# A wait for GpSimd behind VectorE at their shared port, with new durations for the planner and other banks for scores

## The chip, the cores and the metric

The kernel runs on one core of a Trainium2 chip. Five engines work side by side, each on its own queue of instructions: PE (TensorE) multiplies, DVE (VectorE), ACT (ScalarE) and POOL (GpSimd) do elementwise work, SP (SyncE) issues DMAs. The metric is the device time of one execution in microseconds (us); the kernel before took 814.11 us, the median of three runs (812.26 to 815.49).

## The reference

Attention with a causal window of 64 positions over 4 x 8 heads of 576 positions, then a mixture of 4 experts over the 2304 rows that come out. All of it is fp32.

```python
scores = scale * np.matmul(q, k.transpose(0, 1, 3, 2))        # q, k, v: (4, 8, 576, 64)
mask = (rel >= 0) & (rel < window)                            # rel = row - column, window = 64
attn = exp(where(mask, scores, -1e9) - max) / (sum + 1e-9)
x = (attn @ v).transpose(0, 2, 1, 3).reshape(2304, 512)
p = domain_probs / (domain_probs.sum(-1, keepdims=True) + 1e-9)   # (2304, 4)
for e in range(4):                                            # w1: (4, 512, 1024), w2: (4, 1024, 512)
    h = np.maximum(x @ w1[e], 0.0)
    out += p[:, e:e + 1] * (h @ w2[e])
```

## The kernel before, in words

The 2304 rows are cut into 3 groups of 768 rows, and a group's rows into 6 blocks of 128 for attention. The experts' hidden columns are cut into 16 units of 256, so that there are 48 pairs of group and unit (unit 0 to 47). Every fp32 operand of a large product is split in two, a rounded part (`hi`, a cast) and the remainder (`lo`, a subtraction), and three matmuls of the parts stand for one. The remainder is an operation with two inputs from SBUF; it is what DVE and POOL share between them.

The first product of a unit (x times w1) is done as seven products of quarter blocks instead of eight (P1 to P7, six matmuls of 384 columns each, L995), on sums and differences of quarters: B11, B21, B22 and T1 to T4 of a group. Group 0 starts with two units without that (`d`, L1071). The second product (h times w2) is plain in group 0 (`y`, L1189); in groups 1 and 2 it runs over pairs of units with seven products again (tiles `m8P` to `m22P`, L1106), whose weights `wp` are split by ACT (L698) and POOL (L701) and whose inputs `hs` are split at L886 and L889. The last pair is plain again (`z`, L1154).

Attention for a group runs beside the experts of the group before; group 0's attention is the start of the kernel. For a block: scores (`sb`, L367), the row maximum on DVE, the exponentials on ACT, the reciprocal on DVE (tile `st`, L427 and L428), the normalisation (tile `sm`, L434) on POOL or DVE, a transpose (on PE in group 0, by DVE's 32x32 transpose, L455, and a DMA through DRAM later), the product with v (`vb`, L493), and a copy into `xr` (L506).

Order. Nothing is scheduled by hand: each piece of work is a `Step` with a planned duration for every engine that may do it, a due time, the steps that it needs and the buffers that it takes. `Planner.order` plays the steps against these durations, gives each an engine, a start and a buffer, and emits them in order of start. PE's order is mostly fixed beforehand (`seq`). Steps that list an engine under `port` are planned so that DVE and POOL are never at the port at once (`port_free`), but in the program nothing holds POOL to this: a POOL instruction starts as soon as its own inputs are there and POOL is free. An instruction of DVE or POOL keeps its place in its engine's queue.

In PSUM there are eight banks b0 to b7. A score tile of group 0 may take b5, b6, b7, b3, b4, b0 or b1 (kind `pa0`), and the accumulators of the `d` products b0, b1 or b4 (kind `D`). While PE would stand idle by the plan in the first 60 us, filler matmuls (`warm_out`, L1270) are put in, one for each 0.35 us of planned gap.

## Time and profile before

| | us |
|---|---|
| median of 3 runs | 814.11 |
| the profiled execution, whole | 813.13 |
| its span, first to last instruction | 811.3 |
| PE busy / DVE / ACT / POOL in the span | 794.5 / 645.0 / 413.8 / 457.2 |
| mean granted clock of TensorE, as a share | 0.993 |

The profiled execution is 1.0 us below the median, and 1.8 us of it lie outside the span. Times in rows are counted from the span's start. A busy time is the union of an engine's instructions; a matmul's row ends later than the next one's start, since they are pipelined, so the distance of starts shows PE's pace.

### The profile page before, as it was taken

What the parts mean: (1) busy time and instruction counts of PE and PEld (TensorE: products, weight loads), DVE (VectorE), ACT (ScalarE), POOL (GpSimd) and SP (SyncE); (2) the same over time, 40 slices, a digit from 0 to 9 for tenths busy, and PEclk for the clock granted to TensorE, in tenths of its full rate; (3) what the DMA queues carried; (4) which work ended last, traced back from release to release, by engine and by line L of the source; (5) the groups of instructions that cost most, each with busy time, mean ns of one, the idle gap of its engine ahead of it and who ended that gap; (6) DMA issues with size and microseconds to landing.
All of it is one profiled execution on the core that took longest, in us unless ns stands there. A gap on an engine that the chain in (4) does not pass through costs nothing.

```text
span 811.3 us, 14972 instructions
## 1 busy us (share of the span) xinstructions
PE 794.5 (98%) x5256; PEld 746.9 (92%) x5261; DVE 645.0 (79%) x1097; ACT 413.8 (51%) x1031; POOL 457.2 (56%) x426
## 2 busy tenths in 40 slices
PE   8999999999999999999999999998899999999998
PEld 6888988888888888999999999988899999999998
DVE  5897666565756798888988987998899888878884
ACT  6866544454535454665766566584434333334320
POOL 4456867757555234546555544654355767776750
PEclk9999999999999999999999999998999999999999
DMA  9928889888776548786786767564485565655522
GB/s 333 294 80 281 320 283 332 283 286 275 254 269 223 187 169 288 252 278 216 254 278 206 237 220 242 169 201 144 148 271 177 200 198 187 215 191 191 178 84 78
DMA packets 106795, 181.93 MB, mean 224 GB/s; under 512 B 12849, under 2 KB 53217, under 8 KB 106721
## 3 DMA queue, kind: packets, MB, share of 16 engines
q1 hardware_dynamic: 106576, 180.59, 67.5%
q8 instruction: 41, 0.67, 0.3%
q10 hardware_dynamic: 144, 0.39, 0.1%
q14 instruction: 34, 0.27, 0.1%
HBM read 132.16 MB, written 48.78 MB: 223 GB/s over the span
## 4 chain that ended last, share of the span: by engine, by line
PE 88%; DVE 9%; ACT 2%; issue 1%; ACTq 0%; DVEq 0%
PE Y L995 17%; PE y L1189 16%; PE X L995 11%; PE V L995 11%; PE z L1154 2%; PE vb L493 2%; PE sb L367 2%; PE m13P L1106 2%; PE m9P L1106 2%; PE m10P L1106 2%; PE m12P L1106 2%; PE m8P L1106 2%; PE m22P L1106 2%; PE m20P L1106 2%; PE m18P L1106 2%; PE m19P L1106 2%
## 5 line engine op out<-in xcount | busy, mean ns | idle before, releaser
L701 POOL TENSOR_TENSOR wp_P<-wr_P,wp_P 128x512 fp32r<-128x512 f32 x105 | 148.9, 1429 | 77.5 <-ACT wp_P L698 66.9
L1189 PE MATMUL y<-w2s,h 128*128 128x512 f32 x576 | 148.9, 395 | 0.0
L1189 PEld LDWEIGHTS y<-w2s,h 128*128 128x128 f32 x576 | 106.4, 188 | 18.1 <-issue 0.9
L1017 ACT COPY u<-Y 128x384 f32<-128x384 f32 x92 | 44.1, 479 | 123.5 <-PE Y L995 111.5
L698 ACT CAST wp_P<-wr_P 128x512 fp32r<-128x512 f32 x105 | 65.2, 621 | 2.5 <-PE y L1189 1.5
L1014 DVE TENSOR_TENSOR c<-V,u 128x384 f32<-128x384 f32 x46 | 25.8, 561 | 46.9 <-ACT u L1017 46.3
L804 POOL TENSOR_TENSOR w2s<-w2r,w2s 128x512 fp32r<-128x512 f32 x33 | 46.5, 1420 | 23.8 <-ACT w2s L801 21.6
L434 POOL TENSOR_TENSOR sm<-sm,st 128x512 f32<-128x512 f32 x29 | 31.1, 1073 | 50.5 <-DVE st L428 48.3
L995 PE MATMUL Y<-T,w1a 128*128 128x384 f32 x276 | 57.1, 341 | 2.2 <-DVE T L596 1.5
L995 PE MATMUL Y<-T,w1c 128*128 128x384 f32 x276 | 56.7, 340 | 0.9 <-ACT u L1017 0.9
L995 PE MATMUL Y<-T,w1b 128*128 128x384 f32 x276 | 56.5, 341 | 0.6 <-ACT u L1017 0.6
L995 PE MATMUL X<-B,w1c 128*128 128x384 f32 x276 | 56.8, 341 | 0.0
L995 PE MATMUL V<-T,w1b 128*128 128x384 f32 x276 | 56.3, 339 | 0.5 <-DVE h L871 0.5
L995 PE MATMUL X<-B,w1a 128*128 128x384 f32 x276 | 55.5, 335 | 0.2 <-DVE w1a L773 0.2
L995 PE MATMUL V<-B,w1d 128*128 128x384 f32 x276 | 55.6, 336 | 0.2 <-DVE c L1014 0.2
L995 PEld LDWEIGHTS Y<-T,w1a 128*128 128x128 f32 x276 | 48.3, 188 | 5.7 <-DVE T L596 2.2
L995 PEld LDWEIGHTS Y<-T,w1c 128*128 128x128 f32 x276 | 49.6, 191 | 2.7 <-ACT u L1017 1.6
L995 PEld LDWEIGHTS Y<-T,w1b 128*128 128x128 f32 x276 | 49.2, 191 | 2.6 <-ACT u L1017 1.1
L995 PEld LDWEIGHTS V<-T,w1b 128*128 128x128 f32 x276 | 49.1, 188 | 2.3 <-DVE h L871 0.9
L995 PEld LDWEIGHTS X<-B,w1c 128*128 128x128 f32 x276 | 49.7, 191 | 1.4
L995 PEld LDWEIGHTS V<-B,w1d 128*128 128x128 f32 x276 | 48.9, 188 | 1.7 <-DVE c L1014 0.5
L995 PEld LDWEIGHTS X<-B,w1a 128*128 128x128 f32 x276 | 48.6, 188 | 0.5 <-DVE w1a L773 0.5
(583 smaller groups left out, 1973.5 us busy)
## 6 DMA issues: line engine op xcount, KB each, us to landing
wr_P<-kw_P SPq DMA_DIRECT2D x60, 256.0 KB, 4.0
w1a<-kw1a SPq DMA_DIRECT2D x30, 512.0 KB, 4.4
w1b<-kw1b SPq DMA_DIRECT2D x30, 512.0 KB, 3.8
w1c<-kw1c SPq DMA_DIRECT2D x30, 512.0 KB, 3.7
wr_P<-in_moe_w_dram SPq DMA_DIRECT2D x45, 256.0 KB, 4.3
w2r<-in_moe_w_dram SPq DMA_DIRECT2D x36, 256.0 KB, 4.4
vn<-in_v_dram SPq DMA_DIRECT2D x35, 256.0 KB, 5.0
kw1a<-w1a SPq DMA_DIRECT2D x16, 512.0 KB, 3.8
```

Source lines behind the costliest of these rows:

```text
L367: nc.tensor.matmul(ts[i][x * W : (x + 1) * W, p, :], qb.tile[lo:hi, p, x * W : (x + 1) * W], kt.tile[lo:hi, p, x * W : x * W + 2 * W], sta ...
L434: (nc.gpsimd if on == "POOL" else nc.vector).tensor_tensor(out=sm.tile, in0=sm.tile, in1=rl.to_broadcast([P, NP, P]), op=ALU.mult)
L493: nc.tensor.matmul(t[lo:hi, p, x * W : (x + 1) * W], vns[x].tile[:, p * P + lo : p * P + hi], pt_head, start=True, stop=True,)
L698: nc.scalar.copy(make(b, f"wp{pair}_{x}")[:, :, 0], r.tile)
L701: (nc.gpsimd if on == "POOL" else nc.vector).tensor_tensor(out=b.tile[:, :, 1], in0=r.tile, in1=b.tile[:, :, 0].bitcast(F32), op=ALU.subtract)
L804: (nc.gpsimd if on == "POOL" else nc.vector).tensor_tensor(out=b.tile[:, 1], in0=raw.tile, in1=b.tile[:, 0].bitcast(F32), op=ALU.subtract)
L995: nc.tensor.matmul(t[:, :T], wb.tile[:, a, wi, ws], cb.tile[:, x, c, :], start=first and m == 0, stop=m == 5, skip_group_check=True,)
L1014: return lambda on, t, p_: nc.vector.tensor_tensor(out=t, in0=p_, in1=o.tile, op=ALU.add)
L1017: (nc.vector.tensor_copy if on == "DVE" else nc.scalar.copy)(t, p_)
L1106: nc.tensor.matmul(o[:, :T], ww.tile[:, u, a, c * P : (c + 1) * P], hs[i, pname].tile[:, x], start=m == 0 and not onto, stop=m == 5, skip_ ...
L1154: nc.tensor.matmul(o[:, cols], w2p[i][f].tile[:, a, dq * P : (dq + 1) * P], hs[i, name[f, t_]].tile[:, x, cols], start=first and m == 0, s ...
L1189: nc.tensor.matmul(o, hh[:, a, ts], w[:, b], start=x == 0 and m == 0, stop=x == 1 and m == 5)
```

## The change

Four things change. (1) The planned durations: the scores' step on PE goes from 0.55 to 1.15 us, the product with v from 0.62 to 1.25, POOL's splits from 1.2 or 1.25 to 1.29, POOL's other operations and DVE's casts by some hundredths, so that the planner makes another order. (2) The scores of group 0's blocks 3 to 5 take banks of a new kind `pah`: b5, b6, b7 and b4. (3) Where POOL's step at the port was planned later than a DVE step at the port, POOL's first instruction of it now waits until that DVE step has ended. The DVE step taken is the last one whose planned end lies 0.3 us or more ahead of the POOL step's planned start, and the wait is made only if that end is later than the time at which the POOL step's own inputs were planned to be ready. (4) To know the instructions, `nc` is wrapped (`Core`, `Watch`); every DVE and POOL instruction of the kernel then carries the wrapper's line, L34. The arithmetic stays as it was.

```diff
+class Watch:
+    def __init__(self, engine):
+        self.engine, self.made = engine, []
+    def __getattr__(self, name):
+        f = getattr(self.engine, name)
+        def call(*a, **kw):
+            i = f(*a, **kw)
+            self.made.append(i)
+            return i
+        return call
...
+    slots["pah"] = slots["pa"] + ["b4"]
...
     def dvec(n):
-        return 0.1 + 0.00056 * n
+        return 0.13 + 0.00056 * n
     def pool_(n):
-        return 0.1 + 0.00215 * n
+        return 0.18 + 0.00216 * n
...
-        vns, sbs = [Buf(f"vn{n}") for _ in range(2)], [Buf(f"pa{n}") for _ in range(2)]
+        vns, sbs = [Buf(f"vn{n}") for _ in range(2)], [Buf("pah" if n == 0 and 2 * j >= GPB else f"pa{n}") for _ in range(2)]
...
-        s = add(f"S{u}", dict(PE=0.55 + 0.15 * pe_mask), scores, due, [q_dma, k_dma, t_step.get(2 * u - 2) if n else None], sbs, [qb, kt])
+        s = add(f"S{u}", dict(PE=1.15 + 0.2 * pe_mask), scores, due, [q_dma, k_dma, t_step.get(2 * u - 2) if n else None], sbs, [qb, kt])
...
-            l = add(f"wl{pair}{x}", dict(POOL=1.2), lo, due + 0.1, [h], [], [r, b], port=("POOL", "DVE"))
+            l = add(f"wl{pair}{x}", dict(POOL=1.29), lo, due + 0.1, [h], [], [r, b], port=("POOL", "DVE"))
...
+        first = len(nc.gpsimd.made)
+        del nc.vector.made[:]
         s.emit(s.engine)
+        if s.engine == "DVE" and s.port and nc.vector.made:
+            ended.append((s.done, nc.vector.made[-1]))
+        if s.engine == "POOL" and s.port:
+            while len(ended) > 1 and ended[1][0] <= s.start - AHEAD_OF_POOL:
+                ended.pop(0)
+            if ended and ended[0][0] <= s.start - AHEAD_OF_POOL and ended[0][0] > s.ready:
+                tc.add_manual_dep(
+                    nc.gpsimd.made[first].ins, ended[0][1].ins.name, mybir.DependencyInfo(mybir.DependencyClass.Sync, mybir.DependencyReason.DATA),
+                    reason="GpSimd takes its turn at the port",
+                )
...
+AHEAD_OF_POOL = 0.3
```

Of POOL's 400 steps at the port 196 get such a wait: 72 of the 105 `wp` splits, 44 of the weights' sums, the rest spread over the others. Of the DVE steps waited for, 91 are `hs` splits and 20 are DVE's 32x32 transposes. PE's order keeps 687 of its 709 steps in place; what moves is some scores and products with v, and the count of fillers, 22 before and 15 after.

POOL's queue where group 2 begins, before: the end of unit 31's splits, the weights `wp` of pairs 15 and 16, and unit 32's differences (`t32`).

```order
L889 TENSOR_TENSOR hs31P5_7092<-t31P5_7069,hs31P5_7092 128x384 [waits PE_49,Activation_49]
L701 TENSOR_TENSOR wp15_P7_6963<-wr15_P7_6875,wp15_P7_6963 128x2x256 [waits DMAHW0_49]
L701 TENSOR_TENSOR wp15_P5_7048<-wr15_P5_6931,wp15_P5_7048 128x2x256 [waits DMAHW1_49]
L701 TENSOR_TENSOR wp15_P6_7098<-wr15_P6_6986,wp15_P6_7098 128x2x256 [waits DMAHW4_49,PE_49,Activation_49]
L701 TENSOR_TENSOR wp15_P2_7130<-wr15_P2_7041,wp15_P2_7130 128x2x256 [waits DMAHW7_49,PE_49,Activation_49]
L914 TENSOR_TENSOR t32P7_7246<-r3200_7179,r3210_7221 128x384 [waits DVE_49]
L914 TENSOR_TENSOR t32P6_7276<-r3200_7179,t32P5_7263 128x384 [waits DVE_49,Pool_49]
L701 TENSOR_TENSOR wp15_P4_7177<-wr15_P4_7107,wp15_P4_7177 128x2x256 [waits DMAHW2_49,PE_49,Activation_49]
L701 TENSOR_TENSOR wp16_P1_7232<-wr16_P1_7154,wp16_P1_7232 128x2x256 [waits DMAHW3_49,PE_49,Activation_49]
```

The same place of POOL's queue after the change (all rows have the wrapper's line).

```order
L34 TENSOR_TENSOR hs31P7_7066<-t31P7_7051,hs31P7_7066 128x384 [waits DVE_49,PE_49]
L34 TENSOR_TENSOR wp15_P7_6943<-wr15_P7_6864,wp15_P7_6943 128x2x256 [waits DMAHW0_49,DVE_49]
L34 TENSOR_TENSOR wp15_P5_7015<-wr15_P5_6918,wp15_P5_7015 128x2x256 [waits DMAHW1_49,DVE_49,PE_49]
L34 TENSOR_TENSOR wp15_P6_7097<-wr15_P6_6975,wp15_P6_7097 128x2x256 [waits DMAHW4_49,PE_49,Activation_49]
L34 TENSOR_TENSOR wp15_P2_7116<-wr15_P2_7030,wp15_P2_7116 128x2x256 [waits DVE_49,DMAHW7_49,PE_49,Activation_49]
L34 TENSOR_TENSOR t32P6_7259<-r3200_7170,t32P5_7228 128x384 [waits DVE_49]
L34 TENSOR_TENSOR wp15_P4_7167<-wr15_P4_7087,wp15_P4_7167 128x2x256 [waits DVE_49,DMAHW2_49,PE_49,Activation_49]
L34 TENSOR_TENSOR wp16_P1_7223<-wr16_P1_7144,wp16_P1_7223 128x2x256 [waits DMAHW3_49,DVE_49,PE_49]
```

The `wp` splits stand in the same order, and five of the six now wait for DVE too: `wp15_P7` for the end of the second `T4` split, `wp15_P5` for `B22`, `wp15_P2` for `t32P7`, `wp15_P4` for the `hs32P4` split, `wp16_P1` for the `hs32P6` split. The difference `t32P7` has gone from POOL to DVE.

DVE's queue at the same place, before: the last splits of unit 31 and the splits of group 2's quarters, of which PE needs `T2` first.

```order
L914 TENSOR_TENSOR t31P4_7109<-r3101_7067,t31P6_7090 128x384 [waits DVE_49,Activation_49]
L889 TENSOR_TENSOR hs31P7_7080<-t31P7_7064,hs31P7_7080 128x384 [waits Activation_49]
L1120 TENSOR_TENSOR M1P30_4244<-m15P30_7100,M1P30_4244 128x384 [waits PE_49]
L889 TENSOR_TENSOR hs31P4_7119<-t31P4_7109,hs31P4_7119 128x384 [waits Activation_49]
L889 TENSOR_TENSOR hs31P6_7096<-t31P6_7090,hs31P6_7096 128x384
L596 TENSOR_TENSOR T2_2_6978<-T2d0_6802,T2_2_6978 128x384
L596 TENSOR_TENSOR T2_2_6978<-T2d1_6815,T2_2_6978 128x384
L596 TENSOR_TENSOR T3_2_7004<-xr2_4474,T3_2_7004 128x384 x2
```

And after:

```order
L34 TENSOR_TENSOR M1P30_4195<-m15P30_7080,M1P30_4195 128x384 [waits PE_49]
L34 TENSOR_TENSOR t31P4_7107<-r3101_7061,t31P6_7091 128x384 [waits DVE_49]
L34 TENSOR_TENSOR hs31P5_7078<-t31P5_7063,hs31P5_7078 128x384 [waits Activation_49]
L34 TENSOR_TENSOR hs31P6_7105<-t31P6_7091,hs31P6_7105 128x384 [waits Activation_49]
L34 TENSOR_TENSOR hs31P4_7119<-t31P4_7107,hs31P4_7119 128x384 [waits Activation_49]
L34 TENSOR_TENSOR T1_2_6907<-T1d1_6814,T1_2_6907 128x384
L34 TENSOR_TENSOR B21_2_6932<-xr2_4417,B21_2_6932 128x768
L34 TENSOR_TENSOR T2_2_6965<-T2d0_6935,T2_2_6965 128x384
L34 TENSOR_TENSOR T2_2_6965<-T2d1_6947,T2_2_6965 128x384
```

One split of unit 31 has changed places with POOL's (`hs31P7` against `hs31P5`), and the second `T1` split and the `B21` split, which stood earlier on DVE, now stand directly ahead of `T2`.

POOL's queue near the start, where the weights of unit 1 are split, before:

```order
L434 TENSOR_TENSOR sm2_1_483<-sm2_1_483,st2_1_415 128x512 [waits DVE_49]
L773 TENSOR_TENSOR w1c_0_512<-rc0_299,w1c_0_512 128x512 [waits DMAHW6_49,Activation_49]
L560 COPY gate_71<-B21_0_673 1x1 [waits DVE_49]
L773 TENSOR_TENSOR w1a_1_522<-ra1_302,w1a_1_522 128x512 [waits DMAHW7_49,Activation_49]
L773 TENSOR_TENSOR w1c_1_544<-rc1_303,w1c_1_544 128x512 [waits DMAHW0_49,Activation_49]
```

And after:

```order
L34 TENSOR_TENSOR w1c_0_534<-rc0_299,w1c_0_534 128x512 [waits DMAHW6_49,Activation_49]
L34 TENSOR_TENSOR tw0P5_663<-w2r01_390,w2r00_388 128x256 [waits DMAHW2_49,DMAHW1_49]
L34 COPY gate_71<-B21_0_667 1x1 [waits DVE_49]
L34 TENSOR_TENSOR w1a_1_538<-ra1_302,w1a_1_538 128x512 [waits DMAHW7_49,DVE_49,Activation_49]
L34 TENSOR_TENSOR w1c_1_558<-rc1_303,w1c_1_558 128x512 [waits DMAHW0_49,DVE_49,Activation_49]
L34 TENSOR_TENSOR w2s01_704<-w2r01_390,w2s01_704 128x512 [waits DVE_49,Activation_49]
```

The two splits of unit 1's weights now wait for DVE: the first for block 3's second normalisation (`sm3_1`), the second for block 4's first reciprocal. One normalisation (`sm2_1`) has gone from POOL to DVE.

## Rows read from the trace of the kernel before

**Rows 1.** The page's first part: busy us, share of the span, instructions, by engine.

```profile
PE 794.5 (98%) x5256; PEld 746.9 (92%) x5261; DVE 645.0 (79%) x1097; ACT 413.8 (51%) x1031; POOL 457.2 (56%) x426
```

**Rows 2.** Busy us by stretch: PE, PEld, DVE, ACT, POOL; granted clock, DMA share, GB/s.

```profile
0.00:80.00 80.00, 74.72 (x791) 62.30 (x797) 62.58 (x112) 55.36 (x194) 40.84 (x54) 1.00 0.73 245
80.00:280.00 200.00, 200.00 (x1283) 177.52 (x1282) 126.27 (x212) 95.36 (x240) 129.03 (x141) 1.00 0.81 275
...
520.00:580.00 60.00, 53.03 (x269) 50.47 (x269) 53.52 (x81) 32.98 (x71) 28.67 (x22) 0.91 0.51 165
580.00:620.00 40.00, 38.96 (x223) 38.32 (x222) 38.40 (x63) 20.30 (x44) 18.93 (x14) 1.00 0.65 214
620.00:790.00 170.00, 170.00 (x976) 170.00 (x975) 142.43 (x252) 61.79 (x124) 116.03 (x96) 1.00 0.56 182
...
540.00:560.00 20.00, 17.31 (x83) 15.83 (x83) 18.52 (x26) 11.25 (x25) 11.46 (x8) 0.87 0.49 157
560.00:580.00 20.00, 17.24 (x86) 16.92 (x85) 16.41 (x26) 8.13 (x17) 8.35 (x6) 0.88 0.55 190
```

**Rows 3.** PE in order of time: start us, us, what [idle before <-releaser].

```profile
552.95 0.79 PE L995 MATMUL Y<-T,w1a 128*128 128x384 f32 x3 [0.77 <-DVE T L596]
...
555.89 2.29 PE L995 MATMUL Y<-T,w1b 128*128 128x384 f32 x6 [0.57 <-ACT u L1017]
...
561.72 0.68 PE L1106 MATMUL m15P<-hs30P,wp_P 128*128 128x384 f32 x3
...
562.77 1.20 PE L995 MATMUL V<-B,w1d 128*128 128x384 f32 x6
...
575.08 1.22 PE L1106 MATMUL m15P<-hs30P,wp_P 128*128 128x384 f32 x3 [2.76 <-DVE M1P L1120]
...
578.84 0.68 PE L1106 MATMUL m15P<-hs30P,wp_P 128*128 128x384 f32 x3
```

**Rows 4.** DVE in order of time, same columns.

```profile
548.60 2.74 DVE L889 TENSOR_TENSOR hs31P<-t31P,hs31P 128x384 fp32r<-128x384 f32 x2
551.26 3.19 DVE L596 TENSOR_TENSOR T<-T2d,T 128x384 fp32r<-128x384 f32 x2
554.38 1.01 DVE L596 TENSOR_TENSOR T<-xr,T 128x384 fp32r<-128x384 f32 x2
...
568.58 1.65 DVE L914 TENSOR_TENSOR t32P<-r,t32P 128x384 f32<-128x384 f32 x1
```

**Rows 5.** POOL in order of time in the same stretch.

```profile
547.75 6.28 POOL L701 TENSOR_TENSOR wp_P<-wr_P,wp_P 128x512 fp32r<-128x512 f32 x4
...
566.83 6.11 POOL L701 TENSOR_TENSOR wp_P<-wr_P,wp_P 128x512 fp32r<-128x512 f32 x4
```

**Rows 6.** DVE near the start, in order of time, and POOL's split beside it.

```profile
27.71 0.16 DVE L427 TENSOR_SCALAR st<-st 128x4 f32<-128x4 f32 x1
...
28.00 1.31 DVE L427 TENSOR_SCALAR st<-st 128x4 f32<-128x4 f32 x1
...
29.44 2.25 DVE L434 TENSOR_TENSOR sm<-sm,st 128x512 f32<-128x512 f32 x2
...
28.00 1.28 POOL L773 TENSOR_TENSOR w1a<-ra,w1a 128x512 fp32r<-128x512 f32 x1
```

**Rows 7.** PE near the start, in order of time.

```profile
26.08 1.46 PE L1270 MATMUL warm_out<-wide,warm 128*128 128x512 bf16 x6 [0.16 <-DVE B L531]
27.90 1.34 PE L1071 MATMUL d<-B,w1a 128*128 128x384 f32 x6 [0.36 <-ACT sm L395]
```

**Rows 8.** A line's instructions: shortest/median/longest ns, first and last start, form.

```profile
L455 DVE STREAM_TRANSPOSE tp<-sm x24: 694/702/714, 65.3 to 493.7; 128x512 f32<-128x512 f32 x24
...
L903 DVE SCALAR_TENSOR_TENSOR r<-X,pb x32: 540/558/560, 296.8 to 781.5; 128x384 f32<-128x384 f32 x32
```

**Rows 9.** A split of w2 on POOL in group 0 and the product that uses it.

```profile
117.25 2.55 POOL L804 TENSOR_TENSOR w2s<-w2r,w2s 128x512 fp32r<-128x512 f32 x2 [0.43 <-ACT w2s L801]
...
124.04 1.55 PE L1189 MATMUL y<-w2s,h 128*128 128x512 f32 x6
```

More of the change, by code (lines that the diff above doesn't have):

```diff
@@ L21, with __init__, __getattr__ @@
 LATENCY = dict(PE=0.25, ACT=0.12, DVE=0.12, POOL=0.15, SP=1.0)
+class Watch:
[8 more added lines that the diff above has]
+        return call
+class Core:
+    def __init__(self, nc):
+        self.nc, self.vector, self.gpsimd = nc, Watch(nc.vector), Watch(nc.gpsimd)
+    def __getattr__(self, name):
+        return getattr(self.nc, name)
 class Buf:
@@ L135 @@
 def kernel(ctx: ExitStack, tc: tile.TileContext, q, k, v, dprobs, w1, w2, out, out_t):
-    nc = tc.nc
+    nc = Core(tc.nc)
     P = 128
@@ L229 @@
             ALIAS[f"{x}{n}"] = x
-    PSUM = ("X", "Y", "V", "D", "y", "pa", "pa0", "pa1", "pa2", "y1", "ym", "z")
+    PSUM = ("X", "Y", "V", "D", "y", "pa", "pa0", "pa1", "pah", "pa2", "y1", "ym", "z")
     def make(b, name):
@@ L434, in norm @@
                 (nc.gpsimd if on == "POOL" else nc.vector).tensor_tensor(out=sm.tile, in0=sm.tile, in1=rl.to_broadcast([P, NP, P]), op=ALU.mult)
-            nm = add(f"n{uc}", dict(POOL=0.05 + 0.00203 * DM, **(dict(DVE=dve(DM)) if n == 0 else {})), norm, due + 2, [r], [], [sm, st], port=("POOL", "DVE"))
+            nm = add(f"n{uc}", dict(POOL=1.04, **(dict(DVE=dve(DM)) if n == 0 else {})), norm, due + 2, [r], [], [sm, st], port=("POOL", "DVE"))
             if n == 0:
@@ L496, in pv @@
                         )
-        vv = add(f"V{u}", dict(PE=0.62), pv, due + 4, evs + v_dma, [vb], pts + vns)
+        vv = add(f"V{u}", dict(PE=1.25), pv, due + 4, evs + v_dma, [vb], pts + vns)
         if n:
@@ L775 @@
                 h = add(f"{kind}h{i}", dict(ACT=act(m)), hi, due + lo_, [made.get(hi_ - 1, ld)], [b], [part])
-                l = add(f"{kind}l{i}", dict(DVE=dve(m)) if i >= DIRECT else dict(POOL=1.25), lo, due + lo_ + 0.2, [h] + ([fenced] if i == 1 else []), [], [part, b], port=("DVE", "POOL"))
+                l = add(f"{kind}l{i}", dict(DVE=dve(m)) if i >= DIRECT else dict(POOL=1.29), lo, due + lo_ + 0.2, [h] + ([fenced] if i == 1 else []), [], [part, b], port=("DVE", "POOL"))
                 for x in range(lo_, hi_):
@@ L809 @@
             h.gate = ld.gate
-            l = add(f"w2l{i}{f}", dict(POOL=1.25, DVE=dve(DM)) if i < 2 else dict(POOL=1.25), lo2, due + 0.2, [h], [], [raw2, b2], port=("POOL", "DVE"))
+            l = add(f"w2l{i}{f}", dict(POOL=1.29, DVE=dve(DM)) if i < 2 else dict(POOL=1.29), lo2, due + 0.2, [h], [], [raw2, b2], port=("POOL", "DVE"))
             w2_done[i] += [h, l]
@@ L1235 @@
     nc.vector.memset(maskb, 0.0)
-    make_identity(nc, ident)
+    make_identity(tc.nc, ident)
     nc.vector.tensor_copy(identb, ident)
@@ L1264 @@
         LOG.extend(steps)
-    busy = 0.0
+    busy, ended = 0.0, []
     for s in steps:
```

## The prediction

> **What bounds the kernel now.** I read the busy times by engine first, then the same by stretch, then PE's instructions in order of time where PE is not busy, and last DVE and POOL in those stretches. The reader is to see first that PE is busy for 794.5 of 811.3 us [rows 1], so that an engine beside it can give back only what PE waits for. By stretch [rows 2], PE has no idle time between 80 and 280 us and none between 620 and 790; it is idle 5.3 us in the first 80 us, 7.0 us between 520 and 580, and 1.0 us between 580 and 620. Only in 520 to 580 is the granted clock below one: 0.87 and 0.88 over the two stretches of 20 us from 540 on, which is full speed (2.4 GHz) with about 5 us at half (1.2 GHz) in each.
>
> PE's rows there [rows 3] show both losses. It waits for splits of `T` on DVE at 553 us, and then runs slowly: from 555.89 to 561.72, 5.83 us, it starts 18 matmuls (6, 3, 3 and 6), which at the pace of the three and three from 561.72 to 562.77 (1.05 us for six) need 3.15. At 575.08 it has waited 2.76 us for a sum on DVE, and the next 12 matmuls take until 578.84, 3.76 us where 2.10 would do. The slow clock costs 2.7 + 1.7 = 4.4 us, each time behind an idle stretch. With the 7.0 us of waits, this stretch loses 11.4 us.
>
> DVE is late there because of POOL. From 547.75 POOL works on four `wp` splits for 6.28 us without a break, and from 566.83 on four more for 6.11 [rows 5]. Beside them a pair of DVE splits takes 2.74 us and the next pair 3.19, while the same pair just after POOL's last one takes 1.01 [rows 4]: 1.7 and 2.2 us lost on four instructions, and a single difference takes 1.65 in the second run. DVE's row is long while POOL's row lies over it, then DVE gets one operation through, then POOL the next.
>
> Not every DVE row grows so: transposes take 694 to 714 ns and the products read from PSUM 540 to 560, never longer, wherever POOL works [rows 8]. The Trainium skill (SBUF — State Buffer, section SBUF: two separate sides) has the port pair that DVE and GpSimd share as an exclusive lock for a whole instruction, which only DVE operations with two SBUF inputs, or in a mode that uses both ports, take. The trace agrees, and the rule speaks against a part of the change: 20 of the waits are behind DVE transposes, and keep POOL off a port that is free. Were all 20 on the path, at 0.70 us each, the sum would be 14 us worse by it; I find none there.
>
> **The change, part by part.** *The wait, and the order, where group 2 begins.* POOL's five `wp` splits now wait for DVE: `wp15_P7` behind the last `T` split, `wp15_P2`, `wp15_P4` and `wp16_P1` behind unit 32's differences and splits. So the `T2` split that PE waits for at 553 us, and the splits ahead of the sum that it waits for at 575, no longer meet POOL's two runs of four. What is late next? I count DVE's queue from the sum of `m14P3` to the second `T2` split. After the change it has 47 operations of 384 columns, 3 casts, one cast of 768 and 2 splits of 768. Back to back one of 384 costs 0.47 us (a pair 1.01, of which the second row is 0.55 [rows 4]); with 0.3 for a cast, 0.5 for the large cast and 0.9 for a large split (estimates by columns from that 0.47) this is 25 us. PE has 30 steps between the same points, at 1.05 us 31.5 us. POOL has between 9 and 12 operations there, of 1.3 us for 512 columns [rows 6] and, by columns, 1.0 for 384: 10 to 14 us, and those that DVE meets hold it. If DVE met none, `T2` would be 6 us early; if all held it for their whole length, 25 + 14 is 7 us late. Before, the same stretch had 42 operations of 384 instead of 47 and, for the locks, `T2` was late. Much of DVE's queue reads PSUM (20 of the 47), so I take somewhat over half of POOL's 12 us, 7, which makes DVE 32 and PE's wait 1 us. With 1 us for the waits at sums that remain, 2 of the 7.0 us stay: gain 5, between 0 and 6.5. With waits of 1 us I expect the full clock, as between 520 and 540 (the mean of 0.91 over the 60 us is that of 1.0, 0.87 and 0.88 [rows 2]), and 4.0 of the 4.4 us come back (0 to 4.4).
>
> *580 to 620 us.* The 1.0 us idle there is of the same kind, DVE behind runs of POOL splits; the split that starts POOL's run there now waits for one of the differences. Gain 0.8, between 0 and 1.
>
> *The start.* POOL's split of `w1a` at 28.00 lies over a DVE instruction of 1.31 us, whose like takes 0.16, and the next two normalisations take 2.25 [rows 6], where two of this size back to back take 1.3 (twice the 0.47 for 384 columns, by columns). That is 1.15 + 0.95 = 2.1 us of DVE, which PE's transposes and products wait behind, and the change puts POOL's two splits behind these instructions. The banks: at 27.90 the first `d` product starts after fillers since 26.08 and a wait for ACT's exponentials [rows 7], which still read a score bank that `D` needs; scores on `pah` leave b0 and b1 to `d`. At most those 1.8 us come of this, and less if the splits of `B`, which `d` needs too, end later than the bank comes free. What hides the gain: the softmax of six blocks goes through ACT one after another, scores of blocks 3 to 5 now share four banks, so that a block may wait for the one two before it, and two steps of 0.7 us (a normalisation, a copy) come to DVE ahead of `B`. Both ends: 3.9 gained, or 2.0 lost if a block's wait and the two steps lie on the path. I take 1.5 gained, nearer the two locks that the rows show.
>
> *Where the wait costs.* The other waits lie where PE is never idle. Behind a waiting `wp` split stand other splits only, and for these PE waits only if they come later than their lead. The shortest lead in rows is that of a w2 split in group 0, which ends at 119.80 (117.25 + 2.55) and is used at 124.04 [rows 9], 4.2 us. A POOL step held for one DVE operation more is 0.5 to 1 us later. I put this at nothing; the cover is the lead. Fewer fillers (22 to 15) and the handful of scores and `vb` products that move on PE cost nothing while something else sets the pace.
>
> *The sum.* 813.13 (this execution; the runs' median is 1.0 more) - 5.0 - 4.0 - 0.8 - 1.5 = 801.8 us.
>
> **The rivals.** *The port itself is full, so that turns change nothing.* DVE and POOL together are busy for 53.5 + 28.7 = 82 us in the 60 from 520 on [rows 2], and an order doesn't shorten a lock. DVE now has five splits or differences more ahead of `T2` (42 to 47 operations, 2.4 us), and if POOL holds it as long as before, PE's wait at 553 is 2.4 us longer and the clock falls all the same. The start and 580 to 620 still give 2.3: 813.2 us. For it: the long DVE rows. Against it: POOL's run of four, over 6 us, is behind `T2` in the new order, and a third of DVE's busy time reads PSUM.
>
> *POOL held up in group 0, slower.* If a DVE instruction that POOL waits for is itself late (a transpose behind a normalisation, a hidden split behind PE), all of POOL's queue stands, and the w2 splits of the odd units, seven times with a lead of about 4.2 us, come late for `y`. From 4.2 us of delay on PE pays; at 7 us it is 2.8 us seven times, 19.6 us, against a gain of 11.3: 821 us. For it: in group 0 POOL's sums of weights wait behind DVE nearly throughout. Against it: DVE is busy for 126 of 200 us there [rows 2], not enough to be 4 us behind.
>
> *The start goes the wrong way.* With seven fillers fewer, or with scores waiting for a bank, the first products come 2.0 us later instead of 1.5 earlier: 805.3 us. For it: the first 28 us hang together through ACT. Against it: the fillers that go stood where the plan had scores at half their length.
>
> **How the numbers follow.** Chances: 0.69 for the forecast, whose own range is 796 to 807; 0.15 for the full port (810 to 816); 0.10 for the bad start (803 to 809); 0.06 for the held POOL (817 to 825). The predicted time is the forecast's, 801.8. The range from 796 to 811 holds the first and third case and a small part of the second, about eight in ten with what may be wrong in all. A measurement of this kernel tells some 0.5%, 4.1 us, from no change: faster is below 810.0, slower above 818.2. Faster is nearly all of the forecast and of the bad start and a little of the full port, 0.80; the same is most of the full port, 0.13; slower 0.07.
>
> **What would show it.** Right: between 520 and 580 PE's idle time falls to 2 or 3 us with a granted clock of 1.0 in nearly all of it; DVE's `T` splits take 0.5 us each; POOL's `wp` splits begin behind them; the first product of group 2 starts sooner after the first `d`. In the first 80 us, `d` begins near 26 us. Wrong: PE still waits for `T2` for more than 2 us and the clock falls; or idle time of PE between 80 and 280 us behind POOL's w2 splits, which would mean that the waits cost their lead; or a later start of `d`.

## The result, and the profile after

The changed kernel takes 801.15 us (median; 800.65 to 802.02), the kernel before 813.18 beside it: a ratio of 0.985, 95% interval 0.982 to 0.988, some 12 us less. Run again later it took 801.96 (801.03 to 802.01). Forecast were 801.8. The rows below are from the execution of 800.65 us, whose span is 798.9. In the changed kernel all of DVE's and POOL's rows have line L34, so they are told apart by tiles; `P` products are L1023, sums into `m` L1134, `d` L1099, fillers L1298.

Busy time by engine, to be set against [rows 1]:

```profile
PE 786.9 (98%) x5248; PEld 743.2 (93%) x5252; DVE 584.3 (73%) x1084; ACT 423.6 (53%) x1051; POOL 436.5 (55%) x419
```

DVE is busy for 61 us less, with 13 instructions fewer: it stands less at the port. By stretch, with the columns of [rows 2] (PE, PEld, DVE, ACT, POOL, granted clock, DMA share, GB/s):

```profile
0.00:80.00 80.00, 72.92 (x786) 62.01 (x791) 60.59 (x119) 55.62 (x195) 39.54 (x55) 1.00 0.76 255
...
280.00:520.00 240.00, 239.76 (x1633) 231.49 (x1631) 185.33 (x358) 149.41 (x361) 116.83 (x98) 1.00 0.75 236
520.00:580.00 60.00, 58.89 (x345) 57.26 (x342) 52.99 (x102) 38.75 (x83) 27.65 (x22) 1.00 0.59 194
580.00:620.00 40.00, 40.00 (x231) 40.00 (x230) 31.32 (x61) 21.01 (x44) 24.77 (x20) 1.00 0.69 224
620.00:790.00 170.00, 170.00 (x974) 170.00 (x973) 129.48 (x233) 62.35 (x127) 108.38 (x90) 1.00 0.52 169
```

From 520 to 580 PE is idle for 1.1 us instead of 7.0 and the granted clock is 1.00 instead of 0.91; from 580 to 620 the idle 1.0 us is gone; in the first 80 us PE is idle for more than before, 7.1 instead of 5.3, with fewer fillers in it.

PE where it waited for `T2` in [rows 3]; all that is left are two short waits, neither on DVE (the last three rows are for the count of the slow clock further on):

```profile
547.38 1.56 PE L1023 MATMUL X<-B,w1c 128*128 128x384 f32 x6
548.78 1.22 PE L1023 MATMUL Y<-T,w1a 128*128 128x384 f32 x6
550.57 1.31 PE L1023 MATMUL Y<-T,w1b 128*128 128x384 f32 x6 [0.57 <-ACT u L1045]
...
552.62 0.44 PE L1134 MATMUL m15P<-hs30P,wp_P 128*128 128x384 f32 x1 [0.40 <-POOL wp_P L34]
...
554.47 0.68 PE L1134 MATMUL m15P<-hs30P,wp_P 128*128 128x384 f32 x3
...
564.92 0.68 PE L1134 MATMUL m15P<-hs30P,wp_P 128*128 128x384 f32 x3
...
567.01 0.68 PE L1134 MATMUL m15P<-hs30P,wp_P 128*128 128x384 f32 x3
```

DVE and POOL there, against [rows 4, 5]:

```profile
547.65 1.02 DVE L34 TENSOR_TENSOR T<-T2d,T 128x384 fp32r<-128x384 f32 x2
...
549.53 1.02 DVE L34 TENSOR_TENSOR T<-T4d,T 128x384 fp32r<-128x384 f32 x2
```

```profile
550.62 4.76 POOL L34 TENSOR_TENSOR wp_P<-wr_P,wp_P 128x512 fp32r<-128x512 f32 x3 [6.06 <-DVE T L34]
556.49 1.40 POOL L34 TENSOR_TENSOR wp_P<-wr_P,wp_P 128x512 fp32r<-128x512 f32 x1 [1.11 <-DVE t32P L34]
...
561.66 5.47 POOL L34 TENSOR_TENSOR wp_P<-wr_P,wp_P 128x512 fp32r<-128x512 f32 x4 [2.79 <-DVE hs32P L34]
```

POOL stands idle for 6.06 us until the last `T` split is done, and the pair of `T2` splits takes 1.02 us instead of 3.19. POOL's idle time costs PE little: its one wait for a `wp` split is 0.40 us.

Where the time went is read from three points of PE's own rows: the first product of units 4, 30 and 45 (`X<-B,w1a`, one group of six for each unit, in order). The table has them for every kernel below, in us from the start of the span.

| kernel | median us | unit 4 | unit 30 | unit 45 | 30 to 45 |
|---|---|---|---|---|---|
| before | 813.18 | 87.79 | 510.85 | 746.79 | 235.94 |
| changed | 801.15 | 86.98 | 509.85 | 733.74 | 223.89 |
| changed, again (e13) | 801.96 | 88.33 | 511.20 | 735.08 | 223.88 |
| new order and banks, no wait (e1) | 812.45 | 91.23 | 514.82 | 745.52 | 230.70 |
| order before, waits (e2) | 799.55 | 87.46 | 510.02 | 733.42 | 223.40 |
| changed without the new banks (e3) | 804.40 | 92.93 | 515.76 | 739.65 | 223.89 |
| changed, 30 of 196 waits (e4) | 804.89 | 90.45 | 513.94 | 737.82 | 223.88 |
| changed, no waits behind transposes (e6) | 801.60 | 87.74 | 510.60 | 734.45 | 223.85 |
| changed, 47 waits (e7) | 803.08 | 88.14 | 511.76 | 736.14 | 224.38 |
| as e2, with measured DVE and POOL durations (e8) | 800.00 | 87.56 | 509.93 | 733.10 | 223.17 |
| changed, 7 waits (e9) | 805.44 | 90.43 | 514.02 | 738.10 | 224.08 |
| order before, 7 waits (e10) | 804.44 | 90.95 | 514.14 | 740.42 | 226.28 |
| as e1, the wait filled with matmuls (e11) | 811.23 | 90.65 | 514.26 | 744.03 | 229.77 |
| as e8, transposes and reciprocals planned off the port (e12) | 804.46 | 91.50 | 512.41 | 737.30 | 224.89 |

One run of the kernel e6, 1101.22 us at a granted clock of 0.655, is left out of its median. The medians of the kernel before, run beside the experiments, are 814.50 us (for e1 to e4), 811.62 (e6 to e9) and 814.59 (e10 to e13); the ratios below are to these.

Of the 12.4 us by which the changed kernel's span is shorter, 12.05 come between unit 30 and unit 45, and most of that by unit 34 (its first product 584.06 before, 572.28 after); from unit 45 to the end it takes 0.65 us longer than the kernel before (65.16 against 64.51). The start is not to be told from no change: unit 4 begins 0.8 us earlier in one execution and 0.5 later in another of the same kernel. The other kernels have one execution each in the table, so that 1.4 us at unit 4 show nothing by themselves.

### The profile page after: what moved, and what is told of

It is laid out like the page before. It is cut to its first block, busy times and chain, and to the rows that moved or that the text cites. A ratio compares the mean times of both kernels' runs of the same rounds, so it can differ in the third digit from the quotient of the medians.

```text
span 798.9 us, 15007 instructions
## 1 busy us (share of the span) xinstructions
PE 786.9 (98%) x5248; PEld 743.2 (93%) x5252; DVE 584.3 (73%) x1084; ACT 423.6 (53%) x1051; POOL 436.5 (55%) x419
## 4 chain that ended last, share of the span: by engine, by line
PE 91%; DMA 5%; ACT 1%; SPq 1%; DVE 1%; issue 0%; POOL 0%; POOLq 0%
PE Y L1023 18%; PE y L1217 16%; PE V L1023 12%; PE X L1023 11%; PE z L1182 2%; PE vb L521 2%; PE m12P L1134 2%; PE m13P L1134 2%; PE m11P L1134 2%; PE m8P L1134 2%; PE m10P L1134 2%; PE m22P L1134 2%; PE m20P L1134 2%; PE m9P L1134 2%; PE m16P L1134 2%; PE m18P L1134 2%
## 5 line engine op out<-in xcount | busy, mean ns | idle before, releaser
L34 POOL TENSOR_TENSOR wp_P<-wr_P,wp_P 128x512 fp32r<-128x512 f32 x105 | 140.2, 1349 | 93.6 <-ACT wp_P L726 27.9
L34 DVE TENSOR_TENSOR c<-V,u 128x384 f32<-128x384 f32 x46 | 25.9, 562 | 60.2 <-ACT u L1045 60.1
L34 POOL TENSOR_TENSOR w2s<-w2r,w2s 128x512 fp32r<-128x512 f32 x33 | 44.1, 1354 | 26.1 <-ACT w2s L829 13.0
L1023 PE MATMUL Y<-T,w1a 128*128 128x384 f32 x276 | 57.0, 341 | 0.0
L1023 PE MATMUL V<-T,w1b 128*128 128x384 f32 x276 | 56.5, 339 | 0.3 <-DVE h L34 0.2
L1023 PE MATMUL Y<-T,w1c 128*128 128x384 f32 x276 | 55.8, 337 | 0.6 <-ACT u L1045 0.6
L1023 PE MATMUL X<-B,w1c 128*128 128x384 f32 x276 | 56.0, 337 | 0.1
L1023 PE MATMUL Y<-T,w1b 128*128 128x384 f32 x276 | 55.5, 336 | 0.6 <-ACT u L1045 0.6
L1023 PE MATMUL V<-B,w1d 128*128 128x384 f32 x276 | 55.8, 336 | 0.2 <-DVE c L34 0.2
L1023 PE MATMUL X<-B,w1a 128*128 128x384 f32 x276 | 55.4, 335 | 0.0
L34 POOL TENSOR_TENSOR sm<-sm,st 128x512 f32<-128x512 f32 x27 | 30.0, 1112 | 42.7 <-DVE st L34 17.7
L1023 PEld LDWEIGHTS V<-T,w1b 128*128 128x128 f32 x276 | 49.0, 188 | 2.4 <-DVE h L34 0.7
L1023 PEld LDWEIGHTS Y<-T,w1c 128*128 128x128 f32 x276 | 48.9, 188 | 2.1 <-ACT u L1045 0.9
L1023 PEld LDWEIGHTS Y<-T,w1a 128*128 128x128 f32 x276 | 48.7, 188 | 2.3 <-issue 0.2
L1023 PEld LDWEIGHTS Y<-T,w1b 128*128 128x128 f32 x276 | 48.6, 188 | 2.3 <-ACT u L1045 0.9
L1023 PEld LDWEIGHTS X<-B,w1c 128*128 128x128 f32 x276 | 49.1, 188 | 1.7 <-DVE B L34 0.4
L1023 PEld LDWEIGHTS V<-B,w1d 128*128 128x128 f32 x276 | 49.0, 188 | 1.7 <-DVE c L34 0.5
L1023 PEld LDWEIGHTS X<-B,w1a 128*128 128x128 f32 x276 | 48.6, 188 | 0.2 <-DVE h L34 0.2
```

Of the source, the lines that this page charges most:

```text
L34: i = f(*a, **kw)
L1023: nc.tensor.matmul(t[:, :T], wb.tile[:, a, wi, ws], cb.tile[:, x, c, :], start=first and m == 0, stop=m == 5, skip_group_check=True,)
```

## The experiments

The theory: where group 2 begins, POOL's run of `wp` splits no longer lies over DVE's `T` splits, because it waits for its turn. Rivals: the new order alone does it; the waits are needed all along; the banks and the start carry a good part.

**e1: the new order without its waits.** Order and banks of the changed kernel, none of the 196 waits.

```diff
-            if ended and ended[0][0] <= s.start - AHEAD_OF_POOL and ended[0][0] > s.ready:
+            if False and ended and ended[0][0] <= s.start - AHEAD_OF_POOL and ended[0][0] > s.ready:
```

> The changed kernel with none of its 196 waits: the new durations, the new order on every engine and the score banks stay. If the turns at the port are the cause, POOL starts its wp splits as soon as their data are there, runs of four lie over DVE's splits again and PE waits for T2 where group 2 begins: 520 to 580 us has 5 us or more of PE idle time and a granted clock below 0.95, and the time is 809 to 815 us. Rival, the new order alone does it: PE idle there 1 to 2 us, the clock 1.0, the time 800 to 803 us.

Measured: 812.45 us, ratio to before 0.998 (0.997 to 1.000). The run of four and the long DVE rows are back, a product of `V` waits 4.15 us for its `T` split (the second `T1` split, which the new order puts ahead of `T2`), and what follows is slow. From 520 to 580 us PE is idle for 6.6 us, as expected; the granted clock is 0.97 there, not below 0.95:

```profile
520.00:580.00 60.00, 53.41 (x317) 51.48 (x316) 55.29 (x86) 36.10 (x77) 27.95 (x21) 0.97 0.53 179
```

PE, then DVE and POOL where it waits:

```profile
551.89 0.87 PE L1023 MATMUL V<-T,w1b 128*128 128x384 f32 x4
556.91 1.01 PE L1023 MATMUL V<-T,w1b 128*128 128x384 f32 x2 [4.15 <-DVE T L34]
557.72 2.12 PE L1023 MATMUL X<-B,w1c 128*128 128x384 f32 x6
559.64 1.34 PE L1023 MATMUL Y<-T,w1a 128*128 128x384 f32 x6
...
562.70 0.68 PE L1134 MATMUL m15P<-hs30P,wp_P 128*128 128x384 f32 x3
```

```profile
549.16 1.64 DVE L34 TENSOR_TENSOR hs31P<-r,hs31P 128x384 fp32r<-128x384 f32 x1
550.72 1.64 DVE L34 TENSOR_TENSOR t31P<-r,t31P 128x384 f32<-128x384 f32 x1
552.29 0.54 DVE L34 TENSOR_TENSOR M1P<-m15P,M1P 128x384 f32<-128x384 f32 x1
552.75 1.16 DVE L34 TENSOR_TENSOR t31P<-r,t31P 128x384 f32<-128x384 f32 x1
553.84 2.55 DVE L34 TENSOR_TENSOR hs31P<-t31P,hs31P 128x384 fp32r<-128x384 f32 x3
556.32 0.54 DVE L34 TENSOR_TENSOR T<-T1d,T 128x384 fp32r<-128x384 f32 x1
```

```profile
548.78 6.26 POOL L34 TENSOR_TENSOR wp_P<-wr_P,wp_P 128x512 fp32r<-128x512 f32 x4
```

The sum that reads PSUM (`M1P`, 0.54) passes through the middle of the run unhurt; the split and the difference ahead of it take three times the 0.55 they take alone. The waits are the cause: without them the new order and banks bring some 2 us. The parts of that are larger: from unit 30 to 45 it saves 5.2 us, and unit 4 begins 3.4 us later than before.

**e2: the waits on the order before.** The other half: the code of the wait added to the kernel before, whose durations, order and banks stay (182 of POOL's steps get a wait).

```diff
+        if s.engine == "DVE" and s.port and nc.vector.made:
+            ended.append((s.done, nc.vector.made[-1]))
...
+                tc.add_manual_dep(
+                    nc.gpsimd.made[first].ins, ended[0][1].ins.name, mybir.DependencyInfo(mybir.DependencyClass.Sync, mybir.DependencyReason.DATA),
```

> The kernel before with the waits alone: its durations, its order and its banks. If the turns are the cause whatever the order, most of the gain comes back: 801 to 805 us, with PE idle 1 to 3 us in 520 to 580 and the clock at 1.0. Rival, the waits need an order made with measured durations (planned with POOL and PE steps too short, they hold POOL at the wrong places): 808 us or more.

Measured: 799.55 us (798.45 to 799.97), 0.982 (0.979 to 0.984), below what even the theory expected. Between 520 and 580 us:

```profile
520.00:580.00 60.00, 58.50 (x333) 57.54 (x332) 54.76 (x99) 37.89 (x82) 30.40 (x26) 1.00 0.59 199
```

The waits need no order made with measured durations: alone they save 12.5 us between unit 30 and unit 45, more than everything together. The gains of order (5.2) and waits don't add: both shorten the waits of this one stretch. All four runs of this kernel lie below all nine of the changed one, by 0.7 us at least, on another chip or at another time; that is less than my 0.5%. In the profiled executions 0.5 us of it lie between unit 30 and unit 45; why isn't settled.

**e3: the banks of before.** Scores of group 0 on `pa0` again.

```diff
-        vns, sbs = [Buf(f"vn{n}") for _ in range(2)], [Buf("pah" if n == 0 and 2 * j >= GPB else f"pa{n}") for _ in range(2)]
+        vns, sbs = [Buf(f"vn{n}") for _ in range(2)], [Buf(f"pa{n}") for _ in range(2)]
```

> The changed kernel with the scores on the banks of before (pa0, so that D and the scores share b0 and b1). If the start is bound by ACT's softmax chain and not by the bank, nothing changes: 801 us within 1, the first d product within 0.5 us of 26.6. Rival, the bank gave the 1.3 us by which the first d came earlier: d begins near 28 us and the time is 802 to 803.

Measured: 804.40 us (804.18 to 806.10). Both were wrong: the cost is 2.4 to 3.3 us against the changed kernel's two medians. The rows and the table's line are from the slowest of the five executions, 1.7 us above their median. With PE's scores at their measured length the planner puts two steps of transposes ahead of the first `d` product, which then comes 6.8 us later than in the changed kernel:

```profile
25.38 2.76 PE L1298 MATMUL warm_out<-wide,warm 128*128 128x512 bf16 x12
28.87 1.23 PE L471 MATMUL tb<-ident,sm 128*128 128x128 f32 x8 [0.73 <-ACT w2s L829]
29.94 1.03 PE L1298 MATMUL warm_out<-wide,warm 128*128 128x512 bf16 x4
33.39 1.34 PE L1099 MATMUL d<-B,w1a 128*128 128x384 f32 x6 [2.43 <-ACT sm L423]
```

The first `d` waits for ACT's exponentials of the score bank, here for 2.43 us. The stretch of group 2 is untouched (223.89).

**e4: 30 waits.** The changed kernel with only the waits whose step is planned between 530 and 625 us.

```diff
-            if ended and ended[0][0] <= s.start - AHEAD_OF_POOL and ended[0][0] > s.ready:
+            if 530.0 < s.start < 625.0 and ended and ended[0][0] <= s.start - AHEAD_OF_POOL and ended[0][0] > s.ready:
```

> The changed kernel with only those 30 of the 196 waits whose step is planned between 530 and 625 us, where group 2 begins. If the gain sits there alone, the time is that of the changed kernel: 800 to 803 us, with PE idle near 1 us in 520 to 580 and 1 us in 580 to 620. Rival, DVE is late there because it was held in the stretches before, and needs the waits all along: 805 us or more, with PE idle 3 us or more in 520 to 580.

Measured: 804.89 us, 0.989 (0.987 to 0.991): between the two. Group 2 has its whole gain (223.88), so DVE needs no help in the stretches before it; but unit 4 begins at 90.45, 2 to 3.5 us late. The gain doesn't sit in group 2's waits alone: those at the start pay for what the new order costs there (e7 puts them back).

**e9: 7 waits.** Only those of the one pair whose splits met the `T` splits.

```diff
+            if s.name.startswith("wl15P") and ended and ended[0][0] <= s.start - AHEAD_OF_POOL and ended[0][0] > s.ready:
```

> The changed kernel with the waits of one pair's wp splits alone (7 of 196: the pair whose splits met DVE's T splits where group 2 begins). If this one run of POOL is the cause, they bring back most of what the 30 waits of that stretch bring: 805 to 807 us, no PE wait for a T split over 1 us, clock 1.0 from 540 to 580. Rival, other POOL steps (differences, sums, the next pair's splits) fill the port in its place: 809 us or more.

Measured: 805.44 us (805.04 to 806.24). PE's waits between 500 and 640 us (what for: us in total, times, longest):

```profile
PE Y L1023 <- ACT u L1045: 0.6, 1, 0.6
PE m15P L1134 <- POOL wp_P L34: 0.4, 1, 0.4
PE V L1023 <- DVE T L34: 0.2, 1, 0.2
```

7 of 196 waits bring 6.6 of the 6.8 us that all waits bring there, and no other POOL step takes the place of the run.

**e10: the same 7 waits on the kernel before.** As e2, with the condition of e9.

> The kernel before, its durations, order and banks, with 7 waits and nothing else: those of the wp splits of the pair that is split where group 2 begins. If that one run of POOL over DVE's T splits is what the kernel before loses there, nearly all of the 12 us of that stretch come back: 801 to 805 us, with no PE wait for a T split over 1 us and a clock of 1.0 from 540 to 580. Rival, the waits of the stretches before are needed so that DVE is in time: 808 us or more.

Measured: 804.44 us (802.80 to 806.98), 0.989 (0.987 to 0.992): 9.7 of the 12 us between unit 30 and 45 come back, the `T` pairs take 1.01 us, and no product waits for one. The profiled execution, the slowest of the six, loses 3.2 us near the start (`X` waits 2.5 us for a split of `w1a`), which the table's unit 4 shows. Part of what is missing in the stretch lies at its end, where POOL's next runs meet DVE as before and PE is idle for 1.0 us again:

```profile
580.00:620.00 40.00, 38.96 (x222) 38.33 (x221) 39.25 (x63) 19.34 (x41) 20.57 (x15) 1.00 0.72 235
```

**e7: start and group 2.** 47 waits, those planned before 85 us and those of e4.

```diff
+            if (s.start < 85.0 or 530.0 < s.start < 625.0) and ended and ended[0][0] <= s.start - AHEAD_OF_POOL and ended[0][0] > s.ready:
```

> The changed kernel with 47 of its 196 waits: the 17 planned before 85 us and the 30 planned from 530 to 625. If the waits work only at the start and where group 2 begins, the time is the changed kernel's: 800.5 to 802.5 us, although DVE is held elsewhere for 50 us more in all. Rival, the 149 other waits carry part of the gain: 804 us or more.

Measured: 803.08 us (802.72 to 805.07), 1 to 2 us above the changed kernel, half a microsecond outside what was expected. Unit 4 begins at 88.14, as in the changed kernel's second execution. The 149 waits left out bring 0.7 us from unit 4 to 30 and 0.5 from 30 to 45, although DVE is busy for long without them:

```profile
280.00:520.00 240.00, 239.25 (x1608) 229.84 (x1607) 202.64 (x358) 148.14 (x363) 118.08 (x96) 1.00 0.73 236
...
620.00:790.00 170.00, 170.00 (x975) 170.00 (x974) 146.80 (x235) 63.90 (x130) 116.23 (x91) 1.00 0.52 170
```

Against the same stretches of the changed kernel DVE has 17.3 us more in each, and PE's busy time differs by 0.5 us in the first and not at all in the second.

**e8: durations of DVE and POOL alone.** The changed kernel with the old banks (the edit of e3) and two durations of before: the new `dvec`, `pool_`, split and normalisation times stay, PE's scores and `vb` products have their old length.

```diff
-        s = add(f"S{u}", dict(PE=1.15 + 0.2 * pe_mask), scores, due, [q_dma, k_dma, t_step.get(2 * u - 2) if n else None], sbs, [qb, kt])
+        s = add(f"S{u}", dict(PE=0.55 + 0.15 * pe_mask), scores, due, [q_dma, k_dma, t_step.get(2 * u - 2) if n else None], sbs, [qb, kt])
...
-        vv = add(f"V{u}", dict(PE=1.25), pv, due + 4, evs + v_dma, [vb], pts + vns)
+        vv = add(f"V{u}", dict(PE=0.62), pv, due + 4, evs + v_dma, [vb], pts + vns)
```

> The waits on the kernel before, with the measured durations of DVE and POOL, but the old durations of PE's scores and vb products, and the old banks. If the durations of PE's steps alone make the late start that the new banks then mend, this starts like the kernel before or sooner and has the gain of group 2: 798 to 801 us, PE's unit 4 within 1 us of before. Rival, the durations of DVE and POOL make the start late: 803 us or more, with unit 4 3 to 5 us later than before.

Measured: 800.00 us (799.89 to 800.73), unit 4 at 87.56. PE's durations, then, are what makes the start late, and the banks of the change mend only that: with PE's old durations the old banks lose nothing. e3 and e8 differ in these two durations alone; each is one plan, and what is shown is the durations together with the order that they made.

**e6: no waits behind transposes.** The changed kernel without 18 waits that are behind a DVE transpose or reciprocal.

```diff
-            ended.append((s.done, nc.vector.made[-1]))
+            ended.append((s.done, nc.vector.made[-1], s.name[0] in "Tr" and "_" in s.name))
...
-            if ended and ended[0][0] <= s.start - AHEAD_OF_POOL and ended[0][0] > s.ready:
+            if not (ended and ended[0][2]) and ended and ended[0][0] <= s.start - AHEAD_OF_POOL and ended[0][0] > s.ready:
```

> The changed kernel without the 18 of its 196 waits that are behind a DVE transpose or reciprocal. If these operations take no turn at the port, the 18 waits only keep POOL off a free port: PE loses nothing without them, and the time is the changed kernel's 801.2 us or up to 2 us less, all of the difference in the first 280 us. Rival, the wait behind a transpose is what keeps POOL behind the normalisations and casts that follow it in DVE's queue: 803 us or more.

Measured: 801.36, 801.60 and 804.12 us; the ratio is 0.987 (0.983 to 0.990). Unit 4 and unit 45 lie between those of the changed kernel's two executions. The 18 waits neither cost nor bring anything that shows; the experiment does not decide between the theories. By the names of the plan's steps, 13 of the 18 are behind transposes and 5 behind reciprocals. The text ahead of the result gives 20 to transposes; the other 7 of those are behind splits and differences of `T`.

**e12: transposes off the port.** As e8, with the planner told that transposes and reciprocals take no turn at the port.

```diff
-            r = add(f"r{uc}", dict(DVE=0.42), recip, due + 1.8, [e], [], [st], port=("DVE",))
+            r = add(f"r{uc}", dict(DVE=0.42), recip, due + 1.8, [e], [], [st])
...
-                t_step[2 * u + c] = tr = add(f"T{uc}", dict(DVE=0.69), transp, due + 3, [nm], [tb], [sm], port=("DVE",))
+                t_step[2 * u + c] = tr = add(f"T{uc}", dict(DVE=0.69), transp, due + 3, [nm], [tb], [sm])
```

> The kernel with the waits and the measured durations of DVE and POOL alone (800.0 us), its planner told that DVE's transposes and reciprocals take no turn at the port: POOL may be planned beside them and waits behind none. If they do not hold the port, POOL's sums and splits of group 0 start sooner by up to 0.7 us at a transpose, DVE loses nothing, and the time is 798 to 800.5 us. Rival, they hold it like the others: DVE's transposes grow beyond 714 ns beside POOL, and the time is 801.5 us or more.

Measured: 804.46 us (804.04 to 804.72); the time of the rival, and half of its reason. The transposes did not grow (the longest takes 715 ns):

```profile
L34 DVE STREAM_TRANSPOSE tp<-sm 128x512 f32<-128x512 f32 x24 | 16.9, 702 | 2.4 <-DMA wr_P<-in_moe_w_dram 1.2 <-POOL sm L34 0.9 <-DMA pt<-hop 0.2
```

But a reciprocal's step begins with the small `TENSOR_SCALAR` on `st`, and with POOL planned beside it this one grew. All 36 of them, in e8 and then in e12:

```profile
L34 DVE TENSOR_SCALAR st<-st 128x4 f32<-128x4 f32 x36 | 6.8, 188 | 4.1 <-ACT sm L446 2.4 <-ACT sm L423 1.6
L34 DVE TENSOR_SCALAR st<-st 128x4 f32<-128x4 f32 x36 | 16.2, 450 | 3.7 <-ACT sm L446 1.9 <-ACT sm L423 1.6
```

So of the two kinds of step that the edit took off the port, one does lose time beside POOL. How much of the loss this is, is not shown: the plan's order differs from e8's as well, and PE has waits for other DVE steps that e8 did not have or had shorter:

```profile
63.63 0.69 PE L1023 MATMUL X<-B,w1a 128*128 128x384 f32 x1 [2.49 <-DVE h L34]
...
549.60 1.14 PE L1023 MATMUL X<-B,w1a 128*128 128x384 f32 x5 [1.24 <-DVE B L34]
```

Unit 4 begins 3.9 us later than in e8, 1.5 of them are made good by unit 30, and 1.7 are lost from there to unit 45.

**e11: work instead of waiting.** The kernel of e1, with the first matmul of the product that waits repeated.

```diff
+                        if i == 32 and bk == "V" and first and m == 0:
+                            for _ in range(20):
+                                nc.tensor.matmul(
+                                    t[:, :T], wb.tile[:, a, wi, ws], cb.tile[:, x, c, :],
+                                    start=True, stop=False, skip_group_check=True,
+                                )
```

> The changed kernel with none of its waits, and the first matmul of unit 32's V product issued 20 times more, each starting the bank's sum anew (3.5 us at the usual pace), so that PE works while it waits 4.15 us for the T split. If the slow matmuls behind the wait come from the idle time alone, they run at the usual pace (2 products of 6 in 1.2 us each instead of 2.12 and 1.34), the clock is 1.0 from 540 to 580 and the time 1.5 to 2.5 us below that of the kernel without waits (812.45). Rival, they are slow for another reason (the operands): the pace stays and the time is 812 to 814 us.

Measured: 811.23 us (810.73 to 813.83), 1.2 below e1, which ran on another chip; between unit 30 and unit 45 it is 0.9 below. PE:

```profile
551.37 0.34 PE L1023 MATMUL V<-T,w1b 128*128 128x384 f32 x1
551.55 3.68 PE L1029 MATMUL V<-T,w1b 128*128 128x384 f32 x20
555.07 0.69 PE L1023 MATMUL V<-T,w1b 128*128 128x384 f32 x3
556.43 0.62 PE L1023 MATMUL V<-T,w1b 128*128 128x384 f32 x2 [0.68 <-DVE T L34]
556.88 1.56 PE L1023 MATMUL X<-B,w1c 128*128 128x384 f32 x6
558.28 1.22 PE L1023 MATMUL Y<-T,w1a 128*128 128x384 f32 x6
...
561.22 0.68 PE L1140 MATMUL m15P<-hs30P,wp_P 128*128 128x384 f32 x3
```

From 540 to 560 us the granted clock is 1.00, where e1 has 0.91 (e1, then e11):

```profile
540.00:560.00 20.00, 15.85 (x82) 15.20 (x81) 19.32 (x30) 11.09 (x24) 9.67 (x7) 0.91 0.42 145
540.00:560.00 20.00, 18.74 (x103) 17.50 (x101) 19.31 (x30) 11.16 (x25) 9.73 (x7) 1.00 0.41 135
```

The slow clock is a consequence of the idle time, as supposed, but it costs about 1.0 us of PE's rows here (9.85 us from the first matmul of the `V` product, at 551.37, to the next sum into `m`, at 561.22; 10.81 in e1), not 1.5 to 2.5. Of the 2.12 us that e1's `X` product takes, 1.56 stay at full clock; the changed kernel's `X` takes 1.56 at the same place too, and 1.20 on the order before (e2). That part goes with the new order; why isn't shown.

**e13: the changed kernel once more.**

> The changed kernel once more, on the chip of the other three: 801.2 us within 1 by every theory, so that their times can be set against it as well.

Measured: 801.96 us, 0.985 (0.983 to 0.988), on the chip of e10 to e12.

## Why the prediction came out right

*The wait where group 2 begins (5.0 for idle time): right, somewhat more.* Idle time fell from 7.0 to 1.1 us, a gain of 5.9. I left 1 us at `T2` for POOL's holds and 1 us at sums; neither is there. What remains are a wait for ACT's `u` and one for a `wp` split. Of the 7 us that I let POOL hold DVE nearly nothing fell on the `T` splits, since POOL stands still until they are done. e1, e9 and e10 show the mechanism: take the waits away and the run of four and PE's wait are back; put 7 of them back and both are gone, in either order.

*The slow clock (4.0): right.* The granted clock is 1.00 throughout. The 18 and the 12 matmuls whose pace I counted, 5.83 and 3.76 us before, take 3.90 us (550.57 to 554.47, the wait of 0.40 among them) and 2.09 us (564.92 to 567.01) in the changed kernel. Without that wait this is 4.0 us less. e11 shows that the slow pace comes of the idle time ahead of it, at about 1.0 us behind one wait of 4.15. From unit 30's first product to unit 34's the time fell from 73.21 to 62.43 us, 10.8 in all: 5.9 of idle time, 4.0 of clock, and 0.9 that I can't give to single rows.

*580 to 620 us (0.8): right.* The 1.0 us is gone; from unit 34 to unit 45 the time fell by 1.3 us.

*The start (1.5): wrong.* This is the mis-sized term: two executions give -0.5 and +0.8. Both effects that I summed exist. The locks: in e1, POOL's `w1a`, `w1c` and `w2s` lie over a tiny DVE operation and two normalisations, which take 1.24 and 3.33 us; with the waits, 0.14 and 1.26. First DVE in e1, then in the changed kernel:

```profile
28.57 1.24 DVE L34 TENSOR_SCALAR st<-st 128x4 f32<-128x4 f32 x1
...
29.94 3.33 DVE L34 TENSOR_TENSOR sm<-sm,st 128x512 f32<-128x512 f32 x2
```

```profile
27.97 0.14 DVE L34 TENSOR_SCALAR st<-st 128x4 f32<-128x4 f32 x1
...
28.24 1.26 DVE L34 TENSOR_TENSOR sm<-sm,st 128x512 f32<-128x512 f32 x2
```

The four kernels with the new order and no waits before 85 us (e1, e4, e9, e11) begin unit 4 at 90.4 to 91.2; the four with those waits and the new banks (changed twice, e6, e7) at 87.0 to 88.3: about 3 us. And the banks are worth 2.4 to 3.3 us (e3). The step that failed was to count both as gains against the kernel before, with "the handful of scores and `vb` products that move on PE" at nothing. These durations of PE's steps cost as much as locks and banks give: with PE's old durations (e2, e8) the old banks start as early. The locks themselves held up little in the order before: with e2's waits the two rows shrink there too (to 0.14 and 1.26 us), and unit 4 begins only 0.3 us earlier. The first `d` came 1.3 us sooner in the changed kernel (26.57 against 27.90), the sign that I had named; but e2 begins it at 28.75 and reaches unit 4 at 87.46, so that an early `d` alone does not bring an early unit 4. I had a loss, at up to 2.0 us, as the lower end, and took a value nearer the upper. (The plan before has 24 fillers, not 22.)

*The waits elsewhere (nothing): right.* No wait for a w2 split comes of them; the time from unit 4 to unit 30 is 422.87 us in both executions, 423.06 before, and 423.6 in e1 without waits. The rival of a POOL held up in group 0 has no trace, and that of a full port is refuted by e9. For the rule that I weighed against the change, that transposes are free of the port: their durations agree in before, changed, e1, e6 and e12 (680 to 715 ns), and no cost of the waits behind them shows (e6). There are 13 of these waits, not 20, and at 0.70 us each they would be 9 us, not 14. The reciprocals' steps are not free in this way: their small `TENSOR_SCALAR` loses time beside POOL (e12).

So 801.8 came out because the stretch of group 2 gave 10.8 where 9.0 were forecast, and the start about nothing where 1.5 were. The mechanism of group 2 was right; that these two misses offset each other is luck. So is the last microsecond: the sum starts from one execution of the kernel before, whose runs lie between 810.42 and 815.74 us.

## What to carry to other kernels

Look for a run of GpSimd instructions without a break that lies over the VectorE instructions that PE waits for next, and make that run wait for them: here 7 dependencies, on the `wp` splits of one pair of units, were worth some 10 of 12 us. The other 189 take tens of microseconds off DVE, most of them beside a PE that is busy anyway, and bring some 4 us more. The new durations and banks brought nothing on top: the waits alone, on the order before, took 799.55 us. When several edits come together, sum each against the state that the others leave: a bank that frees a wait is no gain if a sibling edit creates that wait.
